# A two-layer MLP behind an attention on one core: the first token block is cut in two along d_ff, weight pieces are loaded into the buffers they end in, and the planner's due times are new

## Chip, cores, metric

The kernel runs on one core of a Trainium2 chip. The metric is the device time of one execution in microseconds. Its engines are TensorE (PE, matmuls; PEld is its weight load), VectorE (DVE), ScalarE (ACT), GpSimd (POOL) and SyncE (SP, which here only issues DMAs).

## What is computed

```python
x = attention(q, k, v)            # 4 batches, 8 heads, 576 positions, head size 64: a pooled attention
                                  # (factor 4, repeated) plus a banded one (|i - j| < 4), summed
x = x.reshape(2304, 512)
h = x @ moe_w_in                  # 512 x 2048
x = (h * sigmoid(h)) @ moe_w_out  # 2048 x 512
h = x @ moe2_w_in                 # second MLP: the same shapes, a rational function of h
return (P(h) / Q(h)) @ moe2_w_out
```

All inputs are fp32. Each MLP product is computed as three matmuls of fp32r operands, high by high, high by low and low by high, so that every weight and every activation is split into a high and a low part.

## The kernel before

**Tiling.** d_ff is cut into 16 pieces f of 128. The 2304 tokens of the first MLP go in five blocks j (`BLOCKS1`, 5, 5, 5, 5 and 4 chunks of 96 tokens). A step is one pair (j, f): an h group of 12 matmuls (`h_mm`, L739, x times a piece of w_in), the activation on ACT and DVE (`th`, `sg`, `gh`, `gl`, L890 to L902), and an o group of 12 matmuls (`o_mm`, L751) that adds to the block's output in the PSUM tiles `acc`. The o group of step s stands behind the h group of step s + 2 at the earliest. `STEP1` lists the steps block by block: all 16 f of block 0, then all 16 of block 1, and so on. After f = 15 `o_out` copies `acc` to the SBUF tiles `xe` and `o_store` writes them to the DRAM buffer `x2s`. The second MLP begins when the fifth block is done.

**Weights.** The weights arrive as raw 32-bit words. `piece` (L636 to L692) loads a raw piece of 512 KB into one of three `raw` buffers and turns it into a high and a low half: `c1` (ACT or DVE) and `c2` (ACT) read the raw words, `c3` (two DVE instructions, L658 and L660), `c4` (an integer add, L664, on DVE or POOL), `c5` (DVE, L667), `c6` (ACT or DVE) and `c7` (a subtraction, L675, DVE or POOL). The 16 pieces I_f of moe_w_in end in tiles `w0` to `w15`, which stay for all blocks. The 16 pieces O_f of moe_w_out end in a ring of three `wo` tiles; each is stored to the DRAM buffer `wos` and loaded from there again in blocks 1 to 4. The 32 pieces of the second MLP end in one `cvo` tile and are stored to `w2s`. In block 0 each step needs two new pieces, in the later blocks none.

**Attention.** The attention of a batch gives six chunks of x. A chunk takes scores (L522, L531), a maximum, exponentials, a sum, a product, transposes (L567), a copy to `PT`, the product with v (L582), an addition that gives `xs` (L589) and a split into `xh` and `xl` (L603). The pooled part of a batch (L423, L457, L471) stands ahead of its chunks. Until the first h group attention may use the PSUM tile `pair` and the two `acc` tiles, afterwards `pair` alone. A block can begin when the `xl` of all its chunks are written.

**Order.** `Plan.run` is a list scheduler that works when the program is built. Each job has a due time, a cost by engine, jobs that it comes after and buffers that it takes and gives. The order in which the jobs start in that plan is the order of the instructions on every engine and of the DMAs on SP's queue. Each queue runs in its order on the chip, and waits only for data and buffers. Due times are fixed numbers: `when[s]` for a step, some 12 us ahead for the loads of its pieces, and `LEAD` (45 us) ahead of a block for all of its attention.

Of the kernel before, what the change touches and what calls it, by code (L numbers as in the profile page):

```python
# [13 lines left out]
I32 = mybir.dt.int32  # L14
# [14 lines left out]
BLOCKS1 = [5, 5, 5, 5, 4]  # L29
BLOCKS2 = [512, 512, 512, 384, 384]  # L30
RING = 3
# [8 lines left out]
LEAD = 45000.0  # L40
# [6 lines left out]
EARLY = 50000.0  # L47
WARM0 = 20
# [6 lines left out]

class Job:
# [20 lines left out]
class Plan:  # L77
# [6 lines left out]
    def __init__(self):  # L84
        self.jobs, self.rings, self.lent = [], {}, {}

    def ring(self, name, n):
        self.rings[name] = list(range(n))

    def add(self, *a, **k):  # L90
        j = Job(*a, **k)
        for u in j.give:
            u.left += 1
        self.jobs.append(j)
        return j

    def run(self):
        users = {}
        for j in self.jobs:
            j.wait = len(j.after)  # L100
# [9 lines left out]
        while events:  # L110
# [16 lines left out]
            pool.sort(key=lambda j: j.due)  # L127
            again = True
            while again:
                again = False  # L130
                for j in pool:
                    if j.ready > t:
                        continue
                    if j.due - j.early > t:
                        heapq.heappush(events, j.due - j.early)
# [80 lines left out]
def tile_kernel(ctx, tc, kq, kqs, vp, vw_in, moe_w_in, moe_w_out, moe2_w_in, moe2_w_out, moe2_a, moe2_b, out):  # L216
# [54 lines left out]
    STEP1 = [(j, f) for j in range(len(BLOCKS1)) for f in range(NF)]  # L271
    when, t = [], HEAD
    for j, f in STEP1:
        when.append(t)
        t += 24 * (BLOCKS1[j] * CH / 2.4 + 14) * PACE

# [16 lines left out]
    plan.lent["pair"] = "acc"  # L293
# [35 lines left out]
    def attention(b):  # L329
        first = chunk_block[b * NCH][0]  # L330
        due0 = when[first * NF] - LEAD
# [11 lines left out]
        for t in range(3):  # L343
# [4 lines left out]
            loads.append(plan.add(f"L{b}{t}", due0 - (9000 if b == 0 else 0) + 100 * t, {"D": 60}, ld, take=[u],  # L348
# [4 lines left out]
        if b == 0:  # L353
            for t in range(3):
                for w in range(2):
# [8 lines left out]
                    sums.append(plan.add(f"R{b}{t}{w}", due0 - 6000, {"V": v_ns(768)}, sm, after=[loads[t]] + sums[:1],  # L364
                                         take=[] if sums else [kdu], give=[kqu[t]]))
            for i in range(2):
                for hf in range(2):
# [15 lines left out]
                    l = plan.add(f"v{b}{i}{hf}", due0 - 7000, {"D": 60}, lv, take=[u], size=HS * 4096)  # L383
                    vs.append(plan.add(f"p{b}{i}{hf}", due0 - 4500, {"G": 2050, "V": 1950}, pv,
                                       after=[l] + vs[:1], take=[] if vs else [vdu], give=[u]))
        else:
# [14 lines left out]
            for f, u, o, n, m in ((ks, kdu, sums, "K", 128 * 4608), (vsum, vdu, vs, "Q", HS * 4096)):  # L401
                j = None
                for r in range(4):
                    j = plan.add(f"{n}{b}{r}", due0 - 14000, {"G": 1000} if r else {"D": 60}, lambda e, f=f, r=r: f(e, r),
                                 after=[j] if j else [], take=[] if j else [u], size=m, margin=500 if r else 0)
                o.append(j)

# [3 lines left out]
        for m in range(2):  # L411
# [3 lines left out]
            d0 = due0 - 3500 + 400 * m  # L415
# [82 lines left out]
        for c in range(NCH):  # L498
            x = {}
            j, i = chunk_block[b * NCH + c]  # L500
            d0 = when[j * NF] - LEAD + 250.0 * i
# [4 lines left out]
            wn = NF - 3 + c // 2  # L506
            if b == 0:
# [62 lines left out]
            def cp_(e, x=x):  # L570
                x["p"] = at.tile([128, 2, 4 * SUB], F32, tag="PT", name="PT", bufs=3)
# [44 lines left out]
            jt = plan.add(f"T{b}{c}", d0, {"P": 500}, tr, after=[jn], take=[pT, pt], give=[eu], margin=MARGIN if b else MARGIN0)  # L616
            jc = plan.add(f"C{b}{c}", d0, {"A": a_ns(384), "V": v_ns(384)}, cp_, after=[jt], give=[pT])
# [7 lines left out]
                plan.add(f"X{b}{c}", d0, {"V": v_ns(384), "G": g_ns(384)}, lo, after=[jh], give=[xu], port=True))  # L625

    xh, xl, x_u, x_first, x_done = {}, {}, {}, {}, {}
# [4 lines left out]
    for name, n in (("raw", 3), ("cw", 3), ("cr", 2), ("cvo", 1), ("wo", RING)):  # L632
        plan.ring(name, n)

    def piece(name, due, src, dst, dst_unit=None, after=None):
# [3 lines left out]
        ru, wu, iu = Unit("raw"), Unit("cw"), Unit("cr")  # L639

        def ld(e):
            x["raw"] = cv.tile([128, DM, 2], I32, tag="raw", name="raw", bufs=3)
# [36 lines left out]
        j1 = plan.add(f"{name}.1", due, {"A": 570, "V": 600}, c1, after=[j0], take=[wu], give=[ru])  # L679
        j2 = plan.add(f"{name}.2", due, {"A": 570}, c2, after=[j0], take=[iu], give=[ru])  # L680
        j3 = plan.add(f"{name}.3", due, {"V": 850}, c3, after=[j1], port=True)
        j4 = plan.add(f"{name}.4", due, {"V": 620, "G": 1270}, c4, after=[j2, j3], port=True)
        j5 = plan.add(f"{name}.5", due, {"V": 620}, c5, after=[j4], give=[ru, iu], port=True)
# [411 lines left out]
```

## Time and profile before

| | us |
|---|---|
| median of 3 runs (934.46 to 936.43) | 934.55 |
| the profiled execution, own time | 939.73 |
| its span, first to last instruction | 937.9 |
| PE busy in the span | 909.9 (97%) |
| DVE busy | 706.6 (75%) |
| ACT busy | 603.0 (64%) |
| POOL busy | 333.6 (36%) |

Matmuls are pipelined and each is recorded with some overlap, so the share of 97% counts more than the array's work: between two matmuls that follow each other at once the profile shows 0.22 us (480 columns), and a mean duration of 0.38 us. How much work PE did in a stretch is better read from the number of matmuls in it. The granted clock is the TensorE clock as a share of its full speed.

### The profile page before, as it was taken

Reading aid. Unit: us, or ns where it says so; the run is one execution under the profiler, and the core shown is the slowest. Engines: PE = TensorE matmul, PEld = TensorE weight load, DVE = VectorE, ACT = ScalarE, POOL = GpSimd, SP = SyncE. Lnnn points to the kernel's source line nnn. Section 1 sums busy time; section 2 is a strip of 40 time slices with the busy share of each in tenths; the row PEclk is TensorE's granted clock in tenths of the full one; section 3 lists DMA queues with packets and bytes.
Section 4 is the critical chain, followed back from the end, with each engine's and each line's share of the span. In section 5 each row is a group of like instructions: output and inputs, shape, how many; then the busy total and the mean of one; then the engine's idle time right before and its main releaser. Section 6 shows DMA issues by size and latency. Waiting matters only on the chain.

```text
span 937.9 us, 16163 instructions
## 1 busy us (share of the span) xinstructions
PE 909.9 (97%) x6201; PEld 762.6 (81%) x6201; DVE 706.6 (75%) x1064; ACT 603.0 (64%) x1214; POOL 333.6 (36%) x279
## 2 busy tenths in 40 slices
PE   8997888999999999999999999999999999999997
PEld 6785666787888778887899988888888888899986
DVE  6899989863457667667332289998999899799995
ACT  4877757644345666555332378877877777788884
POOL 4532232212201132213000046655555546455553
PEclk9999988999999999999999999999999999999999
DMA  9886799688978668774966573002000200200000
GB/s 281 276 232 215 222 294 292 224 316 255 246 247 286 212 227 264 236 289 148 341 216 224 181 287 151 1 1 90 0 1 9 71 1 1 78 1 1 35 1 34
DMA packets 47497, 152.03 MB, mean 162 GB/s; under 512 B 5212, under 2 KB 9948, under 8 KB 47420
## 3 DMA queue, kind: packets, MB, share of 16 engines
q1 hardware_dynamic: 44972, 143.03, 43.8%
q0 software_dynamic: 2160, 7.96, 4.9%
q8 instruction: 49, 0.80, 0.4%
q14 instruction: 28, 0.23, 0.1%
q10 hardware_dynamic: 288, 0.00, 0.0%
HBM read 116.38 MB, written 34.60 MB: 161 GB/s over the span
## 4 chain that ended last, share of the span: by engine, by line
PE 83%; DVE 6%; DMA 5%; ACT 4%; issue 1%; POOL 0%; ACTq 0%; SPq 0%; DVEq 0%; POOLq 0%
PE hps L739 39%; PE acc L965 21%; PE acc L751 17%; DMA raw<-moe_w_in 3%; DMA raw<-moe_w_out 2%; DVE cw L667 1%; ACT E L547 1%; PE wps L250 1%; PE pair L531 1%; PE pair L582 1%; DVE cr L664 1%; ACT EE L439 1%; DVE cw L660 1%; DVE cw L658 1%; PE pair L567 1%
## 5 line engine op out<-in xcount | busy, mean ns | idle before, releaser
L751 PE MATMUL acc<-gh,wo 128*128 128x480 f32 (+1 forms) x640 | 204.8, 378 | 7.0 <-ACT wo L286 3.7
L739 PE MATMUL hps<-xh,w 128*128 128x480 f32 (+1 forms) x640 | 208.1, 384 | 1.0 <-ACT w L286 0.4
L739 PE MATMUL hps<-x2h,wi 128*128 128x512 f32 (+1 forms) x640 | 196.4, 368 | 0.0
L819 POOL TENSOR_TENSOR u<-u,ah 128x512 f32<-128x512 f32 (+1 forms) x80 | 96.1, 1201 | 261.7 <-ACT u L817 260.0
L965 PE MATMUL acc<-wo,gh 128*128 128x512 f32 x576 | 178.0, 390 | 0.0
L751 PEld LDWEIGHTS acc<-gh,wo 128*128 128x128 f32 x640 | 119.0, 188 | 27.5 <-ACT wo L286 5.7
L739 PEld LDWEIGHTS hps<-xh,w 128*128 128x128 f32 x640 | 121.1, 191 | 20.6 <-DVE w L675 1.3
L739 PEld LDWEIGHTS hps<-x2h,wi 128*128 128x128 f32 x640 | 118.9, 188 | 16.4
L996 POOL TENSOR_TENSOR gl<-p,gh 128x512 fp32r<-128x512 f32 (+1 forms) x80 | 120.9, 1511 | 11.6 <-issue 8.8
L965 PEld LDWEIGHTS acc<-wo,gh 128*128 128x128 f32 x576 | 107.7, 188 | 20.9
L739 PE MATMUL hps<-xl,w 128*128 128x480 f32 (+1 forms) x320 | 120.4, 376 | 0.0
L751 PE MATMUL acc<-gl,wo 128*128 128x480 f32 (+1 forms) x320 | 118.5, 370 | 0.0
L739 PE MATMUL hps<-x2l,wi 128*128 128x512 f32 (+1 forms) x320 | 117.7, 368 | 0.0
L965 PE MATMUL acc<-wo,gl 128*128 128x512 f32 x288 | 112.7, 391 | 0.0
L893 DVE SCALAR_TENSOR_TENSOR th<-th,hps 128x480 f32<-128x480 f32 (+1 forms) x80 | 50.4, 629 | 68.4 <-ACT th L890 67.8
L988 DVE SCALAR_TENSOR_TENSOR u<-u,r 128x512 f32<-128x512 f32 (+1 forms) x80 | 99.4, 1243 | 2.8
L890 ACT ACTIVATE th<-hps 128x480 f32<-128x480 f32 (+1 forms) x80 | 44.5, 557 | 87.5 <-PE hps L739 84.8
L981 ACT ACTIVATE r<-u,cst 128x512 f32<-128x512 f32 (+1 forms) x80 | 54.5, 682 | 52.7 <-POOL u L819 52.7
L987 DVE SCALAR_TENSOR_TENSOR u<-u,r 128x512 f32<-128x512 f32 (+1 forms) x80 | 83.5, 1043 | 0.5 <-ACT r L982 0.5
L664 POOL TENSOR_TENSOR cr<-cw,cr 128x512 int32<-128x512 int32 x25 | 33.8, 1353 | 137.4 <-DVE cw L660 96.6
L816 DVE TENSOR_TENSOR p<-p,hps 128x512 f32<-128x512 f32 (+1 forms) x80 | 50.5, 632 | 30.4 <-ACT p L815 30.3
L286 ACT ACTIVATE gh<-th 128x480 fp32r<-128x480 f32 (+1 forms) x79 | 46.6, 590 | 38.6 <-DVE th L893 27.4
(122 smaller groups left out, 1468.8 us busy)
## 6 DMA issues: line engine op xcount, KB each, us to landing
wo<-wos SPq DMA_DIRECT2D x64, 512.0 KB, 4.2
raw<-moe_w_in SPq DMA_DIRECT2D x32, 512.0 KB, 4.7
raw<-moe_w_out SPq DMA_DIRECT2D x32, 512.0 KB, 5.9
w2s<-cvo SPq DMA_DIRECT2D x32, 512.0 KB, 5.6
kq<-kq SPq DMA_DIRECT2D x12, 788.0 KB, 7.8
wos<-wo SPq DMA_DIRECT2D x16, 512.0 KB, 4.7
wi<-w2s SPq DMA_DIRECT2D x16, 512.0 KB, 7.8
wo<-w2s SPq DMA_DIRECT2D x16, 512.0 KB, 7.4
```

Of the source, the lines that this page charges most:

```text
L286: nc.scalar.activation(out, in_, AF.Copy, scale=scale)
L739: nc.tensor.matmul(hps[:, :n], lhsT=wi[:, i, 128 * g:128 * g + 128], rhs=(a, b)[s][:, g, :n], start=(m == 0), stop=(m == len(mms) - 1))
L751: nc.tensor.matmul(acc_t[j][g // 2][:, g % 2, :n], lhsT=wo[:, i, 128 * g:128 * g + 128], rhs=s_[:, :n], start=(f == 0 and m % 3 == 0), sto ...
L816: nc.vector.tensor_tensor(out=p, in0=p, in1=hps, op=ALU.mult)
L819: nc.gpsimd.tensor_tensor(out=u, in0=u, in1=ah, op=ALU.mult)
L890: nc.scalar.activation(x["t"][:, :n], x["h"][:, :n], AF.Tanh, scale=0.5)
L893: nc.vector.scalar_tensor_tensor(out=x["t"][:, :n], in0=x["t"][:, :n], scalar=1.0, in1=x["h"][:, :n], op0=ALU.add, op1=ALU.mult)
L965: nc.tensor.matmul(acc2[j][c], lhsT=a[:, 128 * c:128 * c + 128], rhs=wo[:, i, :], start=(f == 0 and m % 3 == 0), stop=(f == NF - 1 and m % ...
L981: nc.scalar.activation(r, u, AF.Ln, scale=2.0 ** -64, bias=cst[:, 0:1])
L987: nc.vector.scalar_tensor_tensor(out=u, in0=u, scalar=1.000001, in1=r, op0=ALU.add, op1=ALU.mult)
L988: nc.vector.scalar_tensor_tensor(out=u, in0=u, scalar=-2.0, in1=r, op0=ALU.add, op1=ALU.mult)
L996: nc.gpsimd.tensor_tensor(out=gl2[k_][:, :n], in0=p, in1=gh2[k_][:, :n], op=ALU.subtract)
```

## The change

Three things change.

**The order of the first MLP's steps.** `PART1` replaces the loop over blocks: block 0 through f = 0 to 7, then block 1 through f = 0 to 15, then block 0 through f = 8 to 15, then blocks 2, 3 and 4 as before. `first1[f]` is the step that uses piece f first: a step of block 0 for f below 8, of block 1 for the rest. The output of block 0 leaves PSUM twice: the first half is stored to `x2s`, the second half is added to it in DRAM by an accumulating DMA from POOL's queue. All other steps that are not the first with their f load O_f from `wos`, 64 loads in all, as before.

**The buffers.** The rings `raw` (3), `wo` (3) and `cvo` (1) become one ring `buf` of seven tiles of the same size. A raw piece is loaded into the tile in which its halves end: for I_f that is `w{f}`, which is free from the start (or when an early attention load in it has been used), for the others a tile of `buf`. The `xe` tiles come from `buf` too.

**The plan.** Due times are now set by the plan itself: a job without a time of its own gets the earliest of its users' less their costs, `when` is taken from the start times of the plan before, and of six rounds the one with the earliest end on PE is kept. Attention gets due times that are staggered by chunk. The load of O_f, or its reload, comes in the plan after the o group of four steps earlier (`AHEAD`).

```diff
+SPLIT = 8
+AHEAD = 4
-RING = 3
+NBUF = 7
...
+            for d in j.after:
+                d.t = min(d.t, j.t - self.LAT - min(d.cost.values()) -
+                          (d.size / self.DMA_RATE + self.DMA_LAT + PRE if d.size else 0.0))
...
-    STEP1 = [(j, f) for j in range(len(BLOCKS1)) for f in range(NF)]
+    PART1 = [(0, 0, SPLIT), (1, 0, NF), (0, SPLIT, NF)] + [(j, 0, NF) for j in range(2, len(BLOCKS1))]
+    STEP1 = [(j, f) for j, lo, hi in PART1 for f in range(lo, hi)]
+    part1 = [p for p, (j, lo, hi) in enumerate(PART1) for f in range(lo, hi)]
+    first1 = [STEP1.index((0 if f < SPLIT else 1, f)) for f in range(NF)]
...
-    for name, n in (("raw", 3), ("cw", 3), ("cr", 2), ("cvo", 1), ("wo", RING)):
+    for name, n in (("buf", NBUF), ("cw", 3), ("cr", 2)):
...
-            x["raw"] = cv.tile([128, DM, 2], I32, tag="raw", name="raw", bufs=3)
+            if home.ring == "buf":
+                x["raw"] = buf(home, "raw", (128, DM, 2), I32)
+            else:
+                x["raw"] = wp.tile([128, DM, 2], I32, tag=home.ring, name="raw")
...
-            x["hl"] = dst()
+            x["hl"] = dst(home)
...
-        j0 = plan.add(f"{name}.l", due - 12000, {"D": 60}, ld, take=[ru] + ([dst_unit] if dst_unit in wo_u.values() else []),
-                      size=128 * 4096)
+        j0 = plan.add(f"{name}.l", FAR, {"D": 60}, ld, take=[home], size=128 * 4096)
...
-        if f == 0 and lo == 0:
-            acc_t[j] = [ps.tile([128, 2, 512], F32, tag="acc", name="acc", bufs=2) for _ in range(2)]
+        p = part1[s]
+        f0, f1 = PART1[p][1:]
+        if f == f0 and lo == 0:
+            acc_t[p] = [ps.tile([128, 2, 512], F32, tag="acc", name="acc", bufs=2) for _ in range(2)]
...
+        if f0:
+            nc.gpsimd.dma_start(out=o, in_=xe_t[p, i][:, :, :n], accum_op=ALU.add)
+        else:
+            nc.sync.dma_start(out=o, in_=xe_t[p, i][:, :, :n])
...
-                                       after=[wos_job[f], wo_job[NF - 1]], take=[wo_u[s]], size=128 * 4096)
+                                       after=[wos_job[f]], take=[wo_u[s]], size=128 * 4096)
...
+        for s in range(AHEAD, ns):
+            f = STEP1[s][1]
+            j = load_wo[f] if s == first1[f] else wos_load[s]
+            if s - AHEAD in done_o:
+                j.after.append(done_o[s - AHEAD])
...
-    order = plan.run()
+    order = plan.settle(guess, ROUNDS)
```

**The ninth step on TensorE.** Before, the end of the o group with O_6 and the start of the ninth h group; `hps` is the h group's PSUM tile, `xh_759` and `xl_760` are block 0's x, `w8_1552` is piece I_8, `EE0` belongs to the pooled attention of batch 1:

```order
L751 MATMUL acc_1119<-gh_1485,wo_1520 128x480
L457 MATMUL pair_1561<-ident_86,EE0_103 72x48 x12
L751 MATMUL acc_1119<-gh_1485,wo_1520 128x480
L751 MATMUL acc_1119<-gl_1486,wo_1520 128x480
L751 MATMUL acc_1119<-gh_1485,wo_1520 128x480
L739 MATMUL hps_1583<-xh_759,w8_1552 128x480
L739 MATMUL hps_1583<-xl_760,w8_1552 128x480
```

Now, the same place; `xh1_1011` and `xl1_1012` are block 1's x, `w0_717` is piece I_0:

```order
L637 MATMUL pair_1752<-PT_1669,vw_1661 64x48 x16
L821 MATMUL acc_1142<-gh_1695,wo_1682 128x480
L821 MATMUL acc_1142<-gl_1696,wo_1682 128x480
L821 MATMUL acc_1142<-gh_1695,wo_1682 128x480
L821 MATMUL acc_1143<-gh_1695,wo_1682 128x480
L821 MATMUL acc_1143<-gl_1696,wo_1682 128x480
L821 MATMUL acc_1143<-gh_1695,wo_1682 128x480 x2
L821 MATMUL acc_1143<-gl_1696,wo_1682 128x480
L821 MATMUL acc_1143<-gh_1695,wo_1682 128x480
L807 MATMUL hps_1802<-xh1_1011,w0_717 128x480
L807 MATMUL hps_1802<-xl1_1012,w0_717 128x480
```

Ahead of the ninth h group stand 96 matmuls of h and 84 of o in both orders. Its weights were a new piece and are now an old one; its x was there and is now that of block 1, so that the attention of block 1's last chunk (`pair_1752`) has moved ahead of it.

**Raw loads on SP's queue, before.** From the store of O_0 on; `raw<-moe_w_in` is the load of an I piece, `raw<-moe_w_out` of an O piece, `wos<-wo` the store of a finished O piece:

```order
L714 DMA wos_80<-wo_838 128x1024
L397 DMA vd_938<-vp 72x1024
L347 DMA kq_973<-kq 128x1576
L643 DMA raw_1045<-moe_w_out 128x1024
L643 DMA raw_1085<-moe_w_in 128x1024
L714 DMA wos_80<-wo_1098 128x1024
L643 DMA raw_1159<-moe_w_out 128x1024
L643 DMA raw_1216<-moe_w_in 128x1024
L714 DMA wos_80<-wo_1222 128x1024
L643 DMA raw_1241<-moe_w_out 128x1024
L643 DMA raw_1279<-moe_w_in 128x1024
L714 DMA wos_80<-wo_1283 128x1024
```

Now, from the same store on:

```order
L782 DMA wos_80<-wo_747 128x1024
L567 DMA vw_1050<-vw 128x512
L711 DMA raw_1065<-moe_w_out 128x1024
L711 DMA raw_1085<-moe_w_in 128x1024
L711 DMA raw_1114<-moe_w_in 128x1024
L782 DMA wos_80<-wo_1083 128x1024
L711 DMA raw_1221<-moe_w_in 128x1024
L711 DMA raw_1245<-moe_w_out 128x1024
L782 DMA wos_80<-wo_1203 128x1024
L711 DMA raw_1309<-moe_w_in 128x1024
L711 DMA raw_1334<-moe_w_out 128x1024
L782 DMA wos_80<-wo_1311 128x1024
```

Before, one O and one I load stand between two stores, each for a `raw` buffer that an earlier piece has to leave. Now the loads are ahead by one piece of each kind here (ahead of the store of O_1 stood five I and three O loads, now six and four), and none of them needs a buffer that another piece has to leave.

**SP's queue in block 1's second half, now.** From the store of O_8 on; `w2s<-cvo` is the store of a piece of the second MLP:

```order
L782 DMA wos_80<-wo_2234 128x1024
L711 DMA raw_2280<-moe_w_out 128x1024
L791 DMA w2s_82<-cvo_2264 128x1024
L782 DMA wos_80<-wo_2315 128x1024
L711 DMA raw_2344<-moe_w_out 128x1024
L782 DMA wos_80<-wo_2358 128x1024
L711 DMA raw_2379<-moe_w_out 128x1024
L711 DMA raw_2399<-moe2_w_out 128x1024
L711 DMA raw_2451<-moe_w_out 128x1024
L791 DMA w2s_82<-cvo_2401 128x1024
L782 DMA wos_80<-wo_2444 128x1024
L711 DMA raw_2546<-moe_w_out 128x1024
```

The loads of O_11, O_12, O_13, O_14 and O_15 stand here, each behind the store of a piece three or four earlier, which waits until that piece is finished. Before, O_8 to O_15 were loaded in block 0.

## Rows read from the trace of the kernel before

**Rows 1.** Stretches of the span: busy time and instructions by engine, granted clock, DMA.

```profile
0.00:46.40 46.40, 41.35 (x810) 32.23 (x811) 35.47 (x76) 31.84 (x114) 23.65 (x39) 1.00 0.87 277
46.40:101.20 54.80, 47.26 (x316) 35.78 (x316) 51.48 (x94) 39.40 (x91) 16.55 (x14) 1.00 0.74 224
101.20:173.60 72.40, 63.26 (x644) 47.38 (x643) 64.29 (x116) 48.87 (x114) 24.51 (x21) 0.91 0.87 265
173.60:533.50 359.90, 358.38 (x2588) 305.54 (x2587) 199.26 (x361) 173.31 (x384) 55.14 (x46) 1.00 0.74 249
```

**Rows 2.** Stretches, the first product's matmuls alone (line L739), TensorE.

```profile
0.00:101.20 101.20, 23.19 (x96) 1.00 0.80 249
101.20:173.60 72.40, 27.79 (x96) 0.91 0.87 265
```

**Rows 3.** One stretch, the second product's matmuls alone (line L751), TensorE.

```profile
101.20:173.60 72.40, 21.84 (x86) 0.91 0.87 265
```

**Rows 4.** The same stretch, attention's tiles (pair) alone, TensorE.

```profile
101.20:173.60 72.40, 16.66 (x462) 0.91 0.87 265
```

**Rows 5.** Chain of work, 46 to 174 us: shares by line; start, duration, what.

```profile
by line: DMA raw<-moe_w_in 14.8%; DMA raw<-moe_w_out 11.3%; issue 7.8%; DVE cw L667 7.6%; PE hps L739 7.0%; DVE cr L664 5.8%; DVE cw L660 4.8%; DVE cw L658 4.5%; DVE th L893 3.9%; ACT EE L439 2.7%; ACT cw L651 2.6%; DVE w L675 2.0%; DVE n L
121.23 12.20 DMA raw<-moe_w_in
```

**Rows 6.** Chain of work, whole span: one group of 12 matmuls.

```profile
260.16 2.60 PE acc L751 x12
```

**Rows 7.** Groups by shape, TensorE, 101.2 to 173.6 us: count, busy, mean ns, idle before.

```profile
L582 PE MATMUL pair<-PT,vw 54*64 54x48 f32 x192 | 4.1, 222 | 0.7 <-ACT PT L286 0.7
L567 PE MATMUL pair<-ident,E 48*128 48x48 f32 x40 | 2.5, 245 | 3.5 <-DVE xs L589 3.4
L471 PE MATMUL pair<-PT,vd 72*64 72x144 f32 x32 | 2.4, 292 | 0.8 <-ACT PT L286 0.6
L457 PE MATMUL pair<-ident,EE 48*72 48x48 f32 x48 | 1.8, 208 | 1.3 <-ACT EE L439 1.3
```

**Rows 8.** Groups by shape, VectorE, first 540 us.

```profile
L667 DVE SCALAR_TENSOR_TENSOR cw<-raw,cr 128x512 int32<-128x512 int32 x64 | 47.3, 740 | 2.5 <-POOL cr L664 2.2
L893 DVE SCALAR_TENSOR_TENSOR th<-th,hps 128x480 f32<-128x480 f32 x64 | 41.5, 648 | 29.3 <-ACT th L890 28.7
L902 DVE TENSOR_TENSOR gl<-th,gh 128x480 fp32r<-128x480 f32 x54 | 37.8, 700 | 23.4 <-ACT gh L286 23.1
L658 DVE TENSOR_SCALAR cw<-cw 128x512 f32<-128x512 f32 x64 | 28.4, 444 | 13.5 <-ACT cw L651 13.3
L664 DVE CUSTOM_DVE_ANT_0 cr<-cw,cr 128x1024 uint16<-128x1024 uint16 x39 | 27.4, 704 | 0.5
L589 DVE TENSOR_TENSOR xs<-pair,up 128x192 f32<-128x192 f32 x42 | 13.0, 351 | 11.6 <-PE pair L582 11.4
L603 DVE TENSOR_TENSOR xl<-xs,xh 128x384 fp32r<-128x384 f32 x20 | 12.1, 606 | 2.6 <-ACT xh L286 2.4
L556 DVE TENSOR_TENSOR E<-E,r 128x432 f32<-128x432 f32 x12 | 9.4, 779 | 0.0
L675 DVE TENSOR_TENSOR wo<-cw,wo 128x512 fp32r<-128x512 f32 x12 | 8.5, 712 | 0.1
L444 DVE TENSOR_REDUCE r<-EE 128x6 f32<-128x870 f32 x8 | 8.4, 1048 | 0.8 <-ACT EE L439 0.8
```

**Rows 9.** Groups by shape, GpSimd, first 540 us.

```profile
L664 POOL TENSOR_TENSOR cr<-cw,cr 128x512 int32<-128x512 int32 x25 | 33.8, 1353 | 137.4 <-DVE cw L660 96.6 <-ACT th L890 21.2 <-ACT EE L439 6.8
```

**Rows 10.** Timeline, 118 to 119.5 us: start, duration, engine, line, instruction.

```profile
118.16 1.46 POOL L902 TENSOR_TENSOR gl<-th,gh 128x480 fp32r<-128x480 f32 x1 [0.36 <-ACT gh L286]
118.52 1.51 DVE L603 TENSOR_TENSOR xl<-xs,xh 128x384 fp32r<-128x384 f32 x1
```

**Rows 11.** DMA issues: queue, count, KB each, median us to landing.

```profile
raw<-moe_w_out SPq DMA_DIRECT2D x32, 512.0 KB, 5.9
kqd<-kqs POOLq DMA_DIRECT2D x9, 576.0 KB, 8.2
```

More of the change, by code (lines that the diff above doesn't have):

```diff
@@ L47 @@
 EARLY = 50000.0
+ROUNDS = 6
 WARM0 = 20
@@ L84, in __init__, with settle, run @@
     def __init__(self):
-        self.jobs, self.rings, self.lent = [], {}, {}
+        self.jobs, self.sizes, self.lends = [], {}, {}
     def ring(self, name, n):
-        self.rings[name] = list(range(n))
+        self.sizes[name] = n
     def add(self, *a, **k):
         j = Job(*a, **k)
-        for u in j.give:
-            u.left += 1
         self.jobs.append(j)
         return j
-    def run(self):
+    def settle(self, when, rounds):
+        best, tried = None, []
+        for _ in range(rounds):
+            self.run(when)
+            tried.append((max(j.end for j in self.jobs if j.eng == "P"), len(tried), when))
+            when = [j.start for j in self.jobs if j.step is not None]
+        return self.run(min(tried)[2])
+    def run(self, when):
         users = {}
+        self.rings = {k: list(range(n)) for k, n in self.sizes.items()}
+        self.lent = dict(self.lends)
         for j in self.jobs:
+            for u in j.give:
+                u.left = 0
+        for j in self.jobs:
+            j.start = j.end = j.eng = None
+            j.t = when[j.due.step] + j.due.ns
+            for u in j.give:
+                u.left += 1
+        for j in reversed(self.jobs):
+            for d in j.after:
+                d.t = min(d.t, j.t - self.LAT - min(d.cost.values()) -
+                          (d.size / self.DMA_RATE + self.DMA_LAT + PRE if d.size else 0.0))
             j.wait = len(j.after)
@@ L329, in attention @@
     def attention(b):
-        first = chunk_block[b * NCH][0]
-        due0 = when[first * NF] - LEAD
+        d0 = FAR
         kqt, kqu, sums, upt, upu = {}, {}, [], {}, Unit("up")
@@ L347, in ld @@
                 nc.sync.dma_start(out=kqt[t], in_=kq[b, t])
-            loads.append(plan.add(f"L{b}{t}", due0 - (9000 if b == 0 else 0) + 100 * t, {"D": 60}, ld, take=[u],
+            loads.append(plan.add(f"L{b}{t}", FAR, {"D": 60}, ld, take=[u],
                                   size=128 * 4 * 1576))
@@ L363, in sm @@
                         nc.vector.tensor_reduce(out=o, in_=i.rearrange("p g (j r) -> p g j r", r=4), axis=AX.X, op=ALU.add)
[L364 removed]
+                    sums.append(plan.add(f"R{b}{t}{w}", FAR, {"V": v_ns(768)}, sm, after=[loads[t]] + sums[:1],
                                          take=[] if sums else [kdu], give=[kqu[t]]))
@@ L403, in attention @@
                 for r in range(4):
-                    j = plan.add(f"{n}{b}{r}", due0 - 14000, {"G": 1000} if r else {"D": 60}, lambda e, f=f, r=r: f(e, r),
-                                 after=[j] if j else [], take=[] if j else [u], size=m, margin=500 if r else 0)
+                    j = plan.add(f"{n}{b}{r}", FAR, {"G": 1000} if r else {"D": 60}, lambda e, f=f, r=r: f(e, r),
+                                 after=[j] if j else takes[n], take=[] if j else [u], size=m, margin=500 if r else 0)
+                    if r == 0:
+                        takes[n] = [j]
                 o.append(j)
+        if b == 0:
+            takes.update(K=sums[:1], Q=vs[:1])
         ups = []
@@ L506, in attention @@
             wn = NF - 3 + c // 2
+            if b == 0 and c in (3, 4):
+                pt = v0u.setdefault("PT", Unit("w8"))
             if b == 0:
@@ L624, in attention @@
             x_done.setdefault(j, []).append(
-                plan.add(f"X{b}{c}", d0, {"V": v_ns(384), "G": g_ns(384)}, lo, after=[jh], give=[xu], port=True))
+                plan.add(f"X{b}{c}", due, {"V": v_ns(384), "G": g_ns(384)}, lo, after=[jh], give=[xu], port=True))
+    takes = {}
     xh, xl, x_u, x_first, x_done = {}, {}, {}, {}, {}
```

171 lines of the change are left out of this document (101 added, 70 removed).

## The prediction

> **What bounds the kernel now.** I read the span by stretches first [rows 1], cut where TensorE passes three points: its first h group (46.4 us), its ninth (101.2), its seventeenth (173.6); the last cut, 533.5, is the second MLP's first matmul. The reader is to see VectorE's busy time there: 51.5 of 54.8 us in the second stretch, 64.3 of 72.4 in the third, but 199 of 360 in the fourth. PE's own busy time says little, since records overlap. Its work is better counted: 182 matmuls of the MLP in the third stretch [rows 2, 3] at 2.60 us per twelve [rows 6] are 39.4 us, attention's tiles add 16.7 [rows 4], together 56.1 of 72.4. So PE waited 16.3 us there. The granted clock agrees: a mean of 0.91 in that stretch, 1.00 in the others [rows 1]; with the two levels of 1.2 and 2.4 GHz this is about 13 us at the lower one, in a stretch in which PE was waiting.
>
> What it waited for is in the chain of work of 46 to 174 us [rows 5]: raw loads hold 26%, the conversion's lines on DVE most of the rest; PE's h groups hold 7%. One load alone is 12.2 us of the chain. Three `raw` buffers make a circle: `c5` on DVE frees a buffer, SP loads the next piece (5.9 us to land [rows 11]), ACT and DVE convert. Block 0 asks for two pieces per step, and a step takes PE 5.2 us (two groups), while a piece costs DVE 3.0 us (`c3` twice 0.44, `c4` 0.70, `c5` 0.74, `c7` 0.71 [rows 8]) when nothing goes to POOL: 6.1 us for two, and 1.35 us for the activation of the step, before any attention. In block 0 conversion is the slower side, by the rows; from 173.6 on PE is.
>
> **Part by part.** *The new order* asks for 16 pieces in eight steps, as before, then for none of I_0 to I_7 in eight steps and for two per step only from f = 8 of block 1. What it costs is that the x of block 1 must be ready eight steps earlier. I compare the two programs at their ninth h group, ahead of which both have 96 h matmuls and 84 o matmuls.
>
> *DVE ahead of the ninth h group.* Counted in the order, the new program has four more `xl` (0.606), eight more `xs` (0.351), one more reduction and one more product of the pooled part (1.05 each, by L444's row), one more `c5` (0.74), three fewer products on E (0.779), three fewer `c4` (0.704) and one fewer `c7` (0.712): +2.42 +2.81 +2.10 +0.74 -2.34 -2.11 -0.71 = 2.9 us [rows 8]. A few copies go either way and are left out. The last `xl` of block 1 stands just behind the point and is needed: 0.6. At the second stretch's busy share, 51.5/54.8 = 0.94, these 3.5 us take 3.7. The ninth h group, 101.2 before, begins at 105.
>
> *PE.* Attention that now stands ahead of that point: four products with v (4.1/6 = 0.68 each), three transposes of chunks (2.5/5 = 0.50), three of the pooled part (1.8/4 = 0.45) and two products of it (2.4/2 = 1.2) [rows 7]: 2.7 + 1.5 + 1.4 + 2.4 = 8.0 us. They fit into the 54.8 us of the second stretch, where 180 matmuls are 39.0 us of work. So they are done in time in which PE waited.
>
> *Behind it.* Before, 937.9 - 101.2 = 836.7 us follow. Less the 16.3 us of waiting and the 8.0 us of attention, 812.4 remain, if PE no longer waits for weights. Does it? From the ninth h group to the o group of f = 15 in block 1, PE has 34 groups (88.4 us) and some 8 us of attention: 96. DVE has 18 pieces (54.8), 16 activations (0.648 + 0.700, 21.6) and at most 8 us of attention: 84. At the third stretch's busy share, 0.89, these take 95 us. So DVE just keeps up, where it lost before; after that the fourth stretch is as it was. For PE's short waits with DVE so full I add 2 us: the lower bound is 0, the upper 9, by which 84 us at a share of 0.80 outlast PE's 96.
>
> *Loads into their homes* take `raw` out of the chain. I give this no gain of its own: DVE was 94% busy already in the second stretch, and the third stretch's waiting is counted above. It is what makes the assumption of an unbroken DVE plausible.
>
> *Added:* two copies on ACT and two on DVE when block 0's first half leaves PSUM (0.7 each by the nearest row, L902 [rows 8]), hidden because two h groups, 5.2 us, stand between the last o group of one part and the first of the next; without that cover 3 us. Two stores and two accumulating DMAs, which nothing needs before the last block; the nearest row is the accumulating load of attention, 8.2 us to land [rows 11]. Reloads of O pieces are 64 in both. The second MLP is not touched.
>
> The sum: 105 + 812.4 + 2 = 919.4 us of span against 937.9, a gain of 18.5. The profiled execution took 939.73, so 921.2 against that; the median of the runs is 5.2 us below the profiled one, and the gain taken from it gives 934.55 - 18.5 = **916 us**.
>
> **A row that speaks against it.** An `xl` that takes DVE 0.606 in the mean took 1.51 while POOL ran a subtraction that began 0.36 us earlier [rows 10]. Ahead of the ninth h group the new order puts four more `c4` and three more products on E on POOL, against three fewer subtractions and one more. If each of the seven stopped DVE for its whole length, 1.353 us by the longest of these rows [rows 9], 9.5 us would be added: ninth group at 114.5, 925.5 us. I leave this out of the sum, since in the second stretch POOL was busy for 16.6 us and DVE idle for 3.3 [rows 1], so that most of POOL's work lay beside DVE's without a stop. The Trainium skill states in "SBUF — State Buffer", section "Who interferes with whom", that a VectorE instruction with two SBUF inputs and a GpSimd instruction that reads SBUF exclude each other for a whole instruction. The pair in rows 10 agrees with that; how often the two meet is open.
>
> **Rivals.**
> 1. *DMA holds the head.* In the first 46.4 us the queues moved 277 GB/s at a share of 0.87 [rows 1], which is nearly all they give. Ahead of the ninth h group the new order has two more raw loads, three reloads and three more loads of the pooled q and k: 5 x 0.512 + 3 x 0.576 = 4.3 MB [rows 11] (of the other attention loads some come earlier and one later, which about cancels). In the second stretch 224 GB/s ran at a share of 0.74, so at 1.00 there would be room for 54.8 us x 79 GB/s = 4.3 MB: exactly this. If the rate stays at 224, the extra takes 19 us, and the ninth group begins at 120 instead of 105: 931 us. For it: that the room is so just. Against: of the eight extra loads the two raw ones and the reloads are not needed before that point.
> 2. *Slower: SP's order makes a new circle.* In block 1's second half the loads of O_11 and O_15 stand behind the stores of O_8 and O_11, and each store waits until its piece is finished. From O_8 to O_15 there are two rounds of load and conversion. PE has 14 groups, 36.4 us, and some 6 us of attention between their uses: 42 us, 21 per round. A load of 5.9 us and a conversion, for which I take thrice its own 3.0 us on a DVE that has other work between, make 15; with the 12.2 us of the chain's longest load it is 21. From 21 us each microsecond per round costs two; at 32 it is 22 us, more than the gain: 938 us.
> 3. *POOL stops DVE*, as above: 925.5 us.
> 4. *No change:* at its ninth h group PE waits for block 1's x as long as it waited for weights, 18.5 us behind 105; 934.
> 5. *More than forecast:* the early loads take DVE's 3.3 idle us from the second stretch, the 2 us don't come, and the 1.5 us that PE was idle in the fourth stretch [rows 1] go: 909 or less.
>
> **How the numbers follow.** Forecast (909 to 922) 0.56; POOL 0.12; DMA 0.14; slower 0.07; no change 0.04; more 0.07. Less than 0.2% (1.9 us) can't be told from no change here. Faster: 0.56 + 0.12 + 0.14 + 0.07 = 0.89; same 0.04; slower 0.07. The range reaches from half of the better case to most of the DMA case, 907 to 931, and leaves out about 0.04 + 0.05 + 0.04 + 0.07.
>
> **What would show it.** Right: the ninth h group at about 105, the clock at 1.00 from there to the second MLP, the second MLP's first matmul near 515 (533.5 less 18.5), no raw load of note in the chain between 46 and 174 us, DVE at 85 to 90% between 105 and 200. Wrong: a ninth h group behind 115 with the DMA share at 1 or with DVE instructions drawn out beside POOL's (rivals 1 and 3), or PE waiting for `wo` in o groups 17 to 24 behind loads that SP issued late (rival 2).

## The result, and the profile after

The changed kernel takes **925.66 us** (median of 4 runs, 925.09 to 926.58), against 935.11 for the kernel before in the same series (4 runs, 934.46 to 936.43): a ratio of 0.9895, 95% interval 0.988 to 0.991. It is 9.4 us faster, where 18.5 were forecast; 925.66 lies inside the range of 907 to 931, but outside the 909 to 922 that the forecast itself had. The profiled execution took 925.37 us, its span is 923.6.

The stretches of the changed kernel, cut at its first h group (46.9), its second (54.0), its third (about 63), its ninth (112.2), inside its 24th (187.5) and at the second MLP's first matmul (518.8); columns as in [rows 1]:

```profile
0.00:46.90 46.90, 41.99 (x844) 32.82 (x845) 37.26 (x78) 32.61 (x114) 24.85 (x40) 1.00 0.90 284
46.90:54.00 7.10, 3.12 (x15) 2.16 (x12) 7.00 (x16) 4.74 (x15) 2.50 (x3) 0.94 1.00 305
54.00:63.00 9.00, 8.99 (x45) 7.07 (x46) 4.38 (x9) 4.42 (x9) 3.27 (x4) 0.67 0.90 226
63.00:112.20 49.20, 45.97 (x457) 34.72 (x455) 44.36 (x78) 35.10 (x79) 16.83 (x14) 1.00 0.80 242
112.20:187.50 75.30, 75.19 (x393) 64.02 (x394) 61.17 (x104) 45.79 (x87) 17.11 (x14) 1.00 0.80 267
187.50:518.80 331.30, 331.30 (x2617) 279.87 (x2616) 201.66 (x361) 175.59 (x408) 54.72 (x46) 1.00 0.77 258
```

Two things are to be seen. Behind the ninth group PE stands no more: 75.19 of 75.30 us, clock 1.00, where the third stretch of [rows 1] has 0.91. Ahead of it lies a stretch that has no counterpart before: from 54 to 63 us the mean clock is 0.67 (most of it at 1.2 GHz), and DVE and ACT are idle for half of it.

The chain of work between 46 and 188 us, by line, answers to [rows 5]:

```profile
by line: PE hps L807 37.8%; PE acc L821 27.0%; DVE cw L735 3.5%; issue 2.7%; DVE cr L732 2.3%; DVE cw L728 2.2%; ACT cr L723 2.1%; DVE cw L726 1.8%; PE pair L519 1.6%; DVE r L492 1.4%; DVE n L477 1.3%; DVE th L973 1.2%; ACT wo L332 1.2%; DV
```

No raw load is in the row; PE's h and o groups hold 65%, where h groups held 7% and raw loads 26%.

What happened at 54 us is in TensorE's timeline (start, duration, instruction; in brackets the idle time before and what ended it):

```profile
50.61 0.38 PE L807 MATMUL hps<-xh,w 128*128 128x480 f32 x1
54.01 0.77 PE L807 MATMUL hps<-xh,w 128*128 128x480 f32 x1 [3.01 <-DVE th L973]
54.57 0.60 PE L807 MATMUL hps<-xl,w 128*128 128x480 f32 x1
...
59.70 1.39 PE L289 MATMUL wps<-wz 128*128 128x256 bf16 x10
...
61.41 0.48 PE L821 MATMUL acc<-gh,wo 128*128 128x480 f32 x1
```

and in VectorE's:

```profile
50.14 1.98 DVE L735 SCALAR_TENSOR_TENSOR cw<-raw,cr 128x512 int32<-128x512 int32 x2
...
53.31 0.65 DVE L973 SCALAR_TENSOR_TENSOR th<-th,hps 128x480 f32<-128x480 f32 x1
...
59.82 0.65 DVE L973 SCALAR_TENSOR_TENSOR th<-th,hps 128x480 f32<-128x480 f32 x1 [4.34 <-ACT th L970]
```

The second h group waits 3.0 us for `sg` (L973) of the first, which is the last to read the first group's PSUM tile; then its twelve matmuls run from 54.0 to 59.2, twice the 2.60 us of [rows 6], and DVE is idle for 4.3 us until they are through and ACT has read their result. Two tiles of that size exist. The first group has one; the other belongs to the warm-up matmuls (`wps`, line 289), of which ten stand behind the second h group in the new plan. In the kernel before all 169 of them stand ahead of the first, so its second group had a free tile and began at 49.2. The ten take 1.4 us themselves (59.70), in a stretch in which PE does not stand.

### The profile page after: what moved, and what is told of

Its sections match the earlier page's. It is cut to its first block, busy times and chain, and to the rows that moved or that the text cites. A ratio compares the mean times of both kernels' runs of the same rounds, so it can differ in the third digit from the quotient of the medians.

```text
span 923.6 us, 16216 instructions
## 1 busy us (share of the span) xinstructions
PE 906.2 (98%) x6212; PEld 762.3 (83%) x6212; DVE 711.4 (77%) x1060; ACT 606.8 (66%) x1224; POOL 333.2 (36%) x279
## 4 chain that ended last, share of the span: by engine, by line
PE 91%; DVE 4%; ACT 3%; issue 1%; POOL 0%; ACTq 0%; DVEq 0%; POOLq 0%
PE hps L807 43%; PE acc L1054 21%; PE acc L821 21%; PE wps L289 1%; PE pair L637 1%; PE pair L581 1%; PE pair L519 1%; ACT E L597 1%; PE pair L617 1%; DVE cw L735 1%; ACT cr L723 0%; DVE cr L732 0%; ACT PT L332 0%; DVE cw L728 0%; PE pair L471 0%
## 5 line engine op out<-in xcount | busy, mean ns | idle before, releaser
L807 PE MATMUL hps<-xh,w 128*128 128x480 f32 (+1 forms) x640 | 226.0, 381 | 3.6 <-DVE th L973 3.0
L821 PE MATMUL acc<-gh,wo 128*128 128x480 f32 (+1 forms) x640 | 222.8, 376 | 0.0
L1054 PEld LDWEIGHTS acc<-wo,gh 128*128 128x128 f32 x576 | 107.6, 188 | 20.9
L970 ACT ACTIVATE th<-hps 128x480 f32<-128x480 f32 (+1 forms) x80 | 44.5, 557 | 101.7 <-PE hps L807 100.8
L973 DVE SCALAR_TENSOR_TENSOR th<-th,hps 128x480 f32<-128x480 f32 (+1 forms) x80 | 50.4, 631 | 78.9 <-ACT th L970 78.5
L732 POOL TENSOR_TENSOR cr<-cw,cr 128x512 int32<-128x512 int32 x22 | 30.9, 1407 | 135.0 <-DVE cw L728 86.2
```

The costliest lines, as they stand in the source:

```text
L807: nc.tensor.matmul(hps[:, :n], lhsT=wi[:, i, 128 * g:128 * g + 128], rhs=(a, b)[s][:, g, :n], start=(m == 0), stop=(m == len(mms) - 1))
L821: nc.tensor.matmul(acc_t[p][g // 2][:, g % 2, :n], lhsT=wo[:, i, 128 * g:128 * g + 128], rhs=s_[:, :n], start=(f == f0 and m % 3 == 0), st ...
L970: nc.scalar.activation(x["t"][:, :n], x["h"][:, :n], AF.Tanh, scale=0.5)
L973: nc.vector.scalar_tensor_tensor(out=x["t"][:, :n], in0=x["t"][:, :n], scalar=1.0, in1=x["h"][:, :n], op0=ALU.add, op1=ALU.mult)
L1054: nc.tensor.matmul(acc2[j][c], lhsT=a[:, 128 * c:128 * c + 128], rhs=wo[:, i, :], start=(f == 0 and m % 3 == 0), stop=(f == NF - 1 and m % ...
```

## Experiments

The theory to begin with: the new order does what was forecast behind the ninth h group; ahead of it the warm-up tile costs the time. The rivals: DMA, POOL, and a first profiled execution that took longer than usual.

**The kernel before, profiled again** (no edit).

> The kernel before, unchanged, profiled a second time. The first profiled execution took 939.73 us, 4.6 above the median of its runs, and its granted clock between 101 and 174 us had a mean of 0.91. Theory (that execution was an outlier, and the forecast took its extra time for time that the change could save): this one takes 934 to 937 us, its ninth h group begins at 99 to 102 and its seventeenth at 168 to 171, and the 4 us are missing between those two. Rival (every profiled execution is like that): 939 or more, seventeenth at 173 to 174.

It took 933.85 us. Cut at the same points (first, ninth, seventeenth h group, second MLP):

```profile
0.00:45.40 45.40, 40.71 (x812) 31.85 (x812) 35.33 (x76) 31.87 (x114) 23.36 (x39) 1.00 0.86 280
45.40:98.90 53.50, 47.33 (x316) 35.81 (x315) 50.40 (x94) 39.48 (x91) 16.92 (x14) 1.00 0.77 233
98.90:169.40 70.50, 61.28 (x644) 45.78 (x643) 62.50 (x115) 48.33 (x113) 23.34 (x20) 0.95 0.87 269
169.40:527.60 358.20, 358.20 (x2587) 305.48 (x2586) 200.41 (x363) 173.41 (x385) 56.48 (x46) 1.00 0.76 251
```

The first execution took longer than usual, as expected, but its 5.9 us are not all where I put them: 1.0, 1.3, 1.9 and 1.7 us in the four stretches. I compare the others' spans with this one. It is a short one in its turn: 13 runs of the same kernel beside it took 934.50 to 938.33, with a median of 936.31. A gain read against it is too small rather than too large.

**No warm-up matmul behind the first h group**, the rest as changed:

```diff
-    busy = 0.0
+    busy, hs = 0.0, False
...
-            if busy < HEAD + 15000:
+            if busy < HEAD + 15000 and not hs:
                 warm(int((x.start - busy) * WARM_SHARE / 109))
-            busy = x.end
+            busy, hs = x.end, hs or x.step is not None
```

> The changed kernel without the ten warm-up matmuls that stand behind its second h group, nothing else. Theory (they keep the warm-up tile alive, so that the second h group waits 3.0 us for the first one's PSUM tile, after which the clock falls and ACT and DVE stand idle for 4.4 us): second h group at 50 to 51 instead of 54.0, ninth at 105 to 108 instead of 112.2, time 919 to 922. Rival, DMA holds the head: second group earlier, but the ninth still at 111 to 113, time 925 to 926. Rival, POOL stops DVE: the ninth at 110 or later, time 923 to 926.

920.85 us (5 runs, 920.49 to 926.68; ratio 0.9849, 0.9825 to 0.9873, whose interval ends below that of the changed kernel, 0.988 to 0.991). Its stretches, cut at the same groups:

```profile
0.00:48.20 48.20, 42.85 (x845) 33.97 (x845) 37.52 (x79) 32.82 (x114) 24.86 (x40) 0.96 0.89 283
48.20:107.70 59.50, 54.05 (x505) 41.09 (x503) 55.32 (x100) 44.30 (x102) 22.67 (x20) 1.00 0.87 265
107.70:183.00 75.30, 75.19 (x393) 64.03 (x394) 61.15 (x104) 45.85 (x88) 17.46 (x14) 1.00 0.80 268
183.00:514.30 331.30, 331.23 (x2617) 279.86 (x2616) 201.68 (x361) 175.83 (x407) 54.84 (x46) 1.00 0.77 258
```

The second h group follows the first at once (51.7), the clock is 1.00, the ninth begins at 107.7, 4.5 us sooner although the first began 1.3 later; from there on the two kernels are alike to 0.1 us (75.30 and 331.30 in both). So the 4.8 us between the medians come from this place, from the tile and the ten matmuls together. The DMA rival falls too: from the first to the ninth group the changed kernel's queues moved 246 GB/s at a share of 0.83; with PE's wait gone it is 265 at 0.87, and no DMA stands in the chain of work between 46 and 110 us in this run.

**The converse in the kernel before**: ten warm-up matmuls put behind its second h group (`if x.name == "h1.3": warm(10)`).

> The kernel before with ten more warm-up matmuls behind its second h group, nothing else. Theory (a warm-up matmul behind the first h group keeps the warm-up tile alive, so that the second h group must wait for the first one's PSUM tile): the second h group, 49.2 us before, begins at about 51.2, when DVE's sg of the first has ended (50.97), and the third at 55 to 57 instead of 52.5; the ninth is 1 to 4 us later, the time 936 to 939. Rival (the tile doesn't matter, the ten matmuls just fill idle time): second h group at 49.2, ninth at 101, 935.

```profile
47.88 0.38 PE L739 MATMUL hps<-xh,w 128*128 128x480 f32 x1
49.91 0.48 PE L739 MATMUL hps<-xh,w 128*128 128x480 f32 x1 [1.65 <-DVE th L893]
...
52.62 1.27 PE L250 MATMUL wps<-wz 128*128 128x256 bf16 x10
```

In TensorE's timeline the second group now waits 1.65 us for the first one's `sg`, as in the changed kernel; the third is at 54.4 against 51.5, so the wait and the 1.27 us of the ten matmuls both count; the ninth is at 101.5 against 98.9. The median is 939.41 against 936.31 (ratio 1.0037, 1.002 to 1.0053), a little above what I expected. The profiled execution took 934.35, the least of the six, and its span is only 0.6 us longer than that of the kernel before profiled again: 2.0 of the 2.6 us come back behind the ninth group there. Here the wait was shorter and the clock stayed up.

**The old order on the new plan**: the split at 16, the empty part left out.

```diff
-SPLIT = 8
+SPLIT = 16
...
-    PART1 = [(0, 0, SPLIT), (1, 0, NF), (0, SPLIT, NF)] + [(j, 0, NF) for j in range(2, len(BLOCKS1))]
+    PART1 = [(0, 0, SPLIT), (1, 0, NF)] + ([(0, SPLIT, NF)] if SPLIT < NF else []) + [(j, 0, NF) for j in range(2, len(BLOCKS1))]
```

> The changed kernel with the order of before: all 16 steps of block 0, then all of block 1 (its split at 16, the empty third part left out); loads into their homes, seven buffers and the new planner stay. No warm-up matmul stands behind the first h group in it. Theory of the prediction (the order takes the demand for weights out of block 0; homes give nothing of their own): DVE bounds the first 16 steps as before, the seventeenth h group begins at 165 to 172, TensorE's clock falls below 1.00 between 101 and 170, time 930 to 936. Rival (homes, seven buffers and the new plan give most of the gain): seventeenth h group at 152 to 160, time 918 to 927.

933.56 us (7 runs; ratio 0.9972, 0.9961 to 0.9983). Cut at the first, ninth and seventeenth h group:

```profile
43.30:90.50 47.20, 43.49 (x250) 36.20 (x249) 44.49 (x84) 33.30 (x65) 8.00 (x7) 0.96 0.93 283
90.50:165.00 74.50, 65.05 (x669) 49.47 (x669) 66.99 (x120) 52.64 (x127) 24.73 (x21) 0.98 0.80 249
```

DVE is busy for 67.0 of 74.5 us up to the seventeenth group, which begins at 165, PE for 65.1. No DMA stands in the chain of work from 43 to 165 us: the loads into homes take the raw loads out of it, and the time hardly changes. So 0.28% comes from homes, buffers and plan together. This run has no late warm-up, so its counterpart is the 920.85 above: the 12.7 us between them come from the order, with the plan that was made for it.

**DVE and POOL.** On top of the run without late warm-up, the shared products and subtractions all on DVE (`"G"` taken out of the costs of `c4`, `c7`, `no`, `lo` and `gl`).

> The changed kernel without warm-up matmuls behind the first h group, and with the products and subtractions that DVE and POOL share (c4, c7, the chunk's products on E, xl, gl) all on DVE; on POOL stay its DMA issues and the pooled part. Up to the ninth h group about 20 of them, 0.7 us each on DVE and 1.3 on POOL, change engine. Theory (POOL's work lies beside DVE's): DVE gets some 14 us more and has 4 idle, so the ninth h group moves from 107.7 to 116 to 120 and the time from 920.85 to 929 to 935. Rival (each POOL instruction stops DVE for its length): 26 us of stops go, 14 come, the ninth h group at 95 to 100 and 908 to 914 us.

929.37 us (4 runs, 926.96 to 934.01; ratio 0.9905, 0.9876 to 0.9934): POOL's help is worth 5 us by the ratios to the kernel before, 8 by the medians. The profiled execution took 934.01, the most of the four, with a mean clock of 0.85 between the first and the ninth group; in it the ninth is at 120.6, 69.4 us behind the first instead of 59.5. So it does not hold that each POOL instruction stops DVE for its length. That POOL stops DVE at all is not refuted by it. DVE by shape between the first and the ninth h group, with POOL at work:

```profile
L735 DVE SCALAR_TENSOR_TENSOR cw<-raw,cr 128x512 int32<-128x512 int32 x14 | 10.2, 746 | 0.0
L732 DVE CUSTOM_DVE_ANT_0 cr<-cw,cr 128x1024 uint16<-128x1024 uint16 x8 | 6.4, 822 | 0.0
L728 DVE TENSOR_SCALAR cw<-cw 128x512 int32<-128x512 int32 x12 | 6.1, 509 | 0.4
L743 DVE TENSOR_TENSOR w<-cw,w 128x512 fp32r<-128x512 f32 x4 | 4.4, 1090 | 1.5 <-ACT w L332 1.5
```

and without it:

```profile
L732 DVE CUSTOM_DVE_ANT_0 cr<-cw,cr 128x1024 uint16<-128x1024 uint16 x14 | 9.3, 687 | 0.0
L735 DVE SCALAR_TENSOR_TENSOR cw<-raw,cr 128x512 int32<-128x512 int32 x14 | 9.1, 680 | 0.0
L728 DVE TENSOR_SCALAR cw<-cw 128x512 int32<-128x512 int32 x14 | 6.0, 427 | 0.5
L743 DVE TENSOR_TENSOR w<-cw,w 128x512 fp32r<-128x512 f32 x6 | 4.1, 686 | 3.0 <-ACT w L332 2.9
```

These four shapes are drawn out by 14 x 0.066 + 8 x 0.135 + 12 x 0.082 + 4 x 0.404 = 4.6 us, all shapes of the stretch by some 5.7. The single records show how (the run without late warm-up; POOL's instruction, then DVE's beside it):

```profile
54.15 1.29 POOL L743 TENSOR_TENSOR wo<-cw,wo 128x512 fp32r<-128x512 f32 x1 [2.33 <-ACT wo L332]
54.15 0.65 DVE L973 SCALAR_TENSOR_TENSOR th<-th,hps 128x480 f32<-128x480 f32 x1
56.54 1.60 POOL L606 TENSOR_TENSOR E<-E,r 128x432 f32<-128x432 f32 x1
56.82 1.88 DVE L743 TENSOR_TENSOR w<-cw,w 128x512 fp32r<-128x512 f32 x1
102.09 1.35 POOL L732 TENSOR_TENSOR cr<-cw,cr 128x512 int32<-128x512 int32 x1 [2.06 <-DVE cw L728]
102.31 1.41 DVE L728 TENSOR_SCALAR cw<-cw 128x512 int32<-128x512 int32 x1
```

DVE's `w` ends 0.56 us behind POOL's instruction, the `cw` 0.28 behind: they got through only when POOL had ended. DVE's `th`, which reads PSUM, took its usual 0.65 us beside POOL. So a stop is a whole one, but it lasts only for the rest of POOL's instruction, and there are ten such places in the stretch. POOL ran 15 such instructions there, 19.3 us in all; DVE's price for them is about 15 x 0.66 = 10 us, more than the 5.7 that they cost it. In the kernel before the same sum over all shapes gives some 2.3 us, most of it in these two (680 and 427 ns without POOL):

```profile
L667 DVE SCALAR_TENSOR_TENSOR cw<-raw,cr 128x512 int32<-128x512 int32 x13 | 10.3, 794 | 0.0
L660 DVE TENSOR_SCALAR cw<-cw 128x512 int32<-128x512 int32 x13 | 6.1, 473 | 0.4
```

**The homes.** Raw pieces into a ring of three again and from there into their homes; four buffers for the rest instead of seven (seven tiles in all, as before), `AHEAD = 3`. No late warm-up.

```diff
-AHEAD = 4
+AHEAD = 3
...
-NBUF = 7
+NBUF = 4
...
-        j0 = plan.add(f"{name}.l", FAR, {"D": 60}, ld, take=[home], size=128 * 4096)
+        j0 = plan.add(f"{name}.l", FAR, {"D": 60}, ld, take=[ru] + ([] if late else [home]), size=128 * 4096)
...
-        j5 = plan.add(f"{name}.5", FAR, {"V": 620}, c5, after=[j4], give=[iu], port=True)
-        j6 = plan.add(f"{name}.6", FAR, {"A": 530, "V": 360}, c6, after=[j5], port=True)
+        j5 = plan.add(f"{name}.5", FAR, {"V": 620}, c5, after=[j4], give=[ru, iu], port=True)
+        j6 = plan.add(f"{name}.6", FAR, {"A": 530, "V": 360}, c6, after=[j5], port=True, take=[home] if late else [])
```

> The changed kernel without warm-up matmuls behind the first h group, with the pieces loaded into a ring of three raw buffers again and converted from there into their homes; four buffers for the rest instead of seven (as much memory in all), and loads for o at most three steps ahead instead of four. Theory of the prediction (the homes give no time of their own with the new order): ninth h group at 107 to 109, seventeenth at 146 to 149, 920 to 924 us. Rival (three raw buffers make the circle of before again): raw loads in the chain, seventeenth h group at 152 or later, 926 to 934 us.

968.99 us (6 runs; ratio 1.0319, 1.0292 to 1.0347), so neither. Up to the 31st h group it is level or ahead (ninth at 109.6, seventeenth at 146.2, 31st at 230.2 against 237.6); then it falls behind, and the second MLP begins at 562.2 instead of 514.3. The stretch from 260 to 340 us, in which no engine is full:

```profile
260.00:340.00 80.00, 65.08 (x523) 53.36 (x522) 45.68 (x82) 39.17 (x87) 7.25 (x6) 0.83 0.67 214
```

That run changed the raw ring, the number of buffers and `AHEAD` at once. To part the first from the others: **pieces into their homes, but `NBUF = 4` and `AHEAD = 3`.**

> The changed kernel without warm-up matmuls behind the first h group, pieces loaded into their homes, but with four buffers instead of seven and loads for o at most three steps ahead instead of four, as in the run with a raw ring (968.99 us). Theory (not the homes but the few buffers cost that run its 48 us, from the 31st step on): level with that run behind step 30, the second MLP's first matmul at 550 or later, 955 us or more. Rival (loading into a raw ring was what cost it): second MLP at 514 to 522, 920 to 928 us.

975.91 us (4 runs; ratio 1.0423, 1.0377 to 1.0468), second MLP at 570.1. So it is not the raw ring that costs the 50 us, but four buffers with `AHEAD = 3`. By which wait, and which of the two, I did not follow.

**Other splits**, all without late warm-up (8 is the run above).

> The changed kernel without warm-up matmuls behind the first h group, split at 4 instead of 8: block 1 begins at the fifth h group and asks for two pieces per step from the ninth to the twentieth. Theory (a piece costs DVE 3.0 us, a step of two pieces more than PE's 5.2 us, and only what is spread over enough steps is hidden): fifth h group at 76 to 84, ninth at 97 to 101, but PE waits for weights from there, twenty-first at 168 to 176 instead of 166.9, 920 to 928 us. Rival (the earlier the reuse the better): twenty-first h group at 160 to 165, 914 to 919 us.

> The changed kernel without warm-up matmuls behind the first h group, split at 6 instead of 8. Theory (the x of block 1 is ready at about 107 whatever the split, as with the splits at 4 and 8, and a PE that is there sooner waits for it): first h group of block 1 at 102 to 108, the ninth at 107 to 118, 925 to 938 us, between the split at 4 (945.74) and at 8 (920.85). Rival (x is ready sooner when two steps' pieces fewer are needed ahead): first h group of block 1 at 92 to 97, 917 to 922 us.

> The changed kernel without warm-up matmuls behind the first h group, split at 10 instead of 8. Theory (between the splits at 8, 920.85, and at 12, 926.32, since two steps more go at DVE's pace): 921 to 926 us, the eleventh h group 2 to 6 us behind the 116.0 of the split at 8. Rival (with more time for block 1's x the waits of the head go): 915 to 919 us.

> The changed kernel without warm-up matmuls behind the first h group, split at 12 instead of 8: twelve steps ask for two pieces each before block 1 reuses them. Theory (as for the split at 4): these twelve steps go at DVE's pace, the thirteenth h group begins at 130 to 138 instead of 125.1, the twenty-first at 172 to 180, 925 to 932 us, between the split at 8 (920.85) and at 16 (933.56). Rival (any split is as good): 919 to 922.

| split | us (median) | ratio, 95% | first h group of block 1 | second MLP |
|---|---|---|---|---|
| 4 | 945.74 | 1.0066 to 1.0106 | 107.6 | 536.2 |
| 6 | 927.14 | 0.9866 to 0.9936 | 101.7 | 520.3 |
| 8 | 920.85 | 0.9825 to 0.9873 | 107.7 | 514.3 |
| 10 | 927.41 | 0.9871 to 0.9935 | 127.0 | 523.8 |
| 12 | 926.32 | 0.9859 to 0.9905 | 135.5 | 519.7 |
| 16 | 933.56 | 0.9961 to 0.9983 | 165.0 | 525.7 |

The split at 4 shows what I had missed: fewer pieces ahead of block 1 didn't make its x ready sooner. PE is there with four steps less done, at the same 107.6, and four steps of 5.2 us make 20.8 of the 21.9 us by which its second MLP begins later. The end of block 1's attention, in TensorE's timeline:

```profile
92.26 0.68 PE L637 MATMUL pair<-PT,vw 54*64 54x48 f32 x32 [0.81 <-ACT up L332]
94.62 0.68 PE L637 MATMUL pair<-PT,vw 54*64 54x48 f32 x32 [1.68 <-issue]
...
99.37 1.11 PE L637 MATMUL pair<-PT,vw 54*64 54x48 f32 x32 [0.58 <-ACT PT L332]
104.23 1.11 PE L637 MATMUL pair<-PT,vw 54*64 54x48 f32 x32 [3.75 <-issue]
107.57 0.77 PE L807 MATMUL hps<-xh,w 128*128 128x480 f32 x1 [2.23 <-ACT xh L332]
```

and in SP's queue:

```profile
93.00 0.40 SPq L567 DMA_DIRECT2D vw<-vw  x1
93.50 0.40 SPq L840 DMA_DIRECT2D x2s<-xe  x1
95.35 0.33 SPq L567 DMA_DIRECT2D vw<-vw  x1
```

Four products with v come 2 to 5 us apart. The loads of `vw` are issued just as a product ends (92.94 and 95.30), since there are two buffers: this looks like attention at the pace of product, load, product, but it is argued: the last product waits 3.75 us for something that the profile doesn't name, and that it is its load, no row shows. The split at 6 came out as expected but for its 101.7, just ahead of the 102 I gave, the split at 12 as expected. The split at 10 came out worse than I expected, at 927.41 instead of 921 to 926 (the profiled execution took 929.99, the most of its four): its seventh h group begins at 96.1, 22 us behind its sixth, with attention ahead of it on PE. Each split is a new plan, so these are six plans, not a curve.

## Why the prediction was half right

**The order, behind the ninth group: right.** I forecast that 836.7 us there become 814.4, a gain of 22.3. The changed kernel has 923.6 - 112.2 = 811.4. Against the execution profiled again (931.9 - 98.9 = 833.0) this is a gain of 21.6, against the first, from which I forecast, 25.3; that the 21.6 lies so near is in part luck. The run with the old order shows that it is the order, with its plan: without it 933.56. The work that I gave DVE from there to the o group of f = 15 in block 1 was 84 us; it measured 85.9, and its share between 105 and 200 us was 0.85, at the lower end of the 0.85 to 0.90 I gave:

```profile
112.20:214.10 101.90, 101.79 (x678) 84.33 (x678) 85.92 (x149) 67.66 (x145) 26.40 (x21) 1.00 0.80 270
105.00:200.00 95.00, 94.38 (x589) 78.70 (x590) 80.59 (x139) 60.07 (x126) 23.23 (x19) 1.00 0.82 276
```

So conversion kept up, and the 2 us for short waits didn't come: PE stood for 0.1 us of the 101.9.

**"The ninth h group, 101.2 before, begins at 105": wrong; 112.2.** This is the step that failed: I let the order cost 3.8 us ahead of that point, it cost 13.3 (112.2 against 98.9; 11.0 against the first execution). The span shows it whole: 21.6 - 13.3 = 8.3 us gained (931.9 to 923.6; the second MLP's start, 404.8 us from the end against 404.3, has no part). Two terms stood at nothing in my sum.

The first is the warm-up tile. I had counted PE's and DVE's instructions ahead of that group, but took no notice that ten warm-up matmuls had changed their place. They cost 4.5 us, by the run without them: the wait for the tile that they held, the low clock behind it and their own 1.4 us, which no run parts.

The second is POOL's stops, "I leave this out of the sum". My reason was that DVE was idle for 3.3 us only; but a stopped DVE instruction is a longer record and counts as busy, so idle time can't show it. In the run without late warm-up 8.8 us of the 13.3 are left, 2.8 at the first h group (48.2 instead of 45.4; over the kernels here it lies between 43.3 and 51.2) and 6.0 behind it. Up to its ninth group DVE was busy for 92.8 us against 85.7 in the kernel before. Of these 7.1 us some 4.0 are records drawn out beside POOL (5.7 against 2.3 behind the first group, 0.6 ahead of it), and the other 3.1 are near the 2.9 that I counted. At DVE's share of 0.87 the 7.1 us take 8.2 of the 8.8. This is an estimate, since no run took the stops away and left DVE its work.

With the ten matmuls out of the way the span is 919.1, near the 919.4 forecast, but that is chance: the forecast started from an execution 6.0 us longer, and against the second one the gain is 12.8, not 18.5.

**"I give this no gain of its own" (loads into homes): right for the time, too narrow in what it saw.** With the old order, homes, buffers and plan give 0.28%. But with four buffers and `AHEAD = 3` the kernel is some 50 us slower, and the seven take the place of the seven tiles in the old rings; what they would cost beside a raw ring of three, no run shows.

**The rivals.** DMA: 246 GB/s up to the ninth group, 265 when PE no longer waited, and no DMA in the chain; not it. POOL: 925.5 us, within 0.2 us of the result, but as a sum this is luck. The mechanism is there, at some 4.0 us of DVE's time instead of 9.5, and 4.5 us of the result come from the ten matmuls. A price near the measured time is no evidence. SP's circle at O_8 to O_15 did not come: from 112.2 to 520 us the profile names a single wait of PE, of 0.4 us. The second MLP's first matmul is at 518.8 where I gave 515: of the 7.2 us at the ninth group 3.8 are left there.

## What to carry to other kernels

When a schedule is made anew, look through its order for every instruction that has moved across a tile's last use, not only those that cost time: ten idle-time matmuls, 1.4 us of work, held one of two PSUM tiles and cost 4.8 us in all. Price a neighbour's stops by single records against the same shape alone, since a stop counts as busy time. A gain behind a point and a loss ahead of it are two terms with two errors; here the first held to 0.7 us (3.0 by the first execution) and the second was off by 9.5 (7.2). And an early start of the next block is worth only as much as that block's own input is early: in the plans with fewer than eight steps ahead the split bought nothing, since x was ready at 102 to 108 us anyway.

## What was not expected of the hardware

A wait of 3.0 us on PE at 51 us was followed by 1.2 GHz for most of 54 to 63 us (mean 0.67), so the second group took 5.17 us instead of 2.60; a wait of 1.65 us at the same place in the other kernel was followed by matmuls at full speed. Two executions of one program also differ: the kernel before took 933.85 in one profile and 939.73 in the other, with a mean clock of 0.95 and 0.91 in its third stretch. Beside POOL, some of DVE's instructions end 0.28 to 0.56 us behind POOL's, as if they began there (1.88 us instead of 0.69, 1.41 instead of 0.43); others, which read PSUM, take as long as alone. Over a whole shape this is 0.07 to 0.40 us in the mean, which hides how long a single stop is.
